# Unsigned conversion on ScalarE in place of a logical shift on VectorE, in the weight conversion of an attention and mixer kernel

## The chip, the cores and the metric

The kernel runs on one core of a Trainium2 chip (trn2). The metric is device time in microseconds of one execution, as the median over runs. Five engines work side by side, each with its own queue of instructions in a fixed order: TensorE (PE, with its weight loads as PEld), VectorE (DVE), ScalarE (ACT), GpSimd (POOL) and SyncE (SP, which here only issues DMAs).

## The reference, cut to what matters

Causal attention with a cumulative bias (4 batches, 8 heads, 576 positions, head size 64) feeds a gated feed-forward layer, and that a mixer over tokens and channels. What matters here are the seven large weight arrays.

```
x = attention(q, k, v, s)                       # (4, 576, 512)
xk, xr = mixes of x and x shifted by one row    # mu_k, mu_r
kk = relu(xk @ w_k) ** 2                        # w_k  512 x 1024
x  = sigmoid(xr @ w_r) * (kk @ w_v)             # w_r  512 x 512, w_v 1024 x 512
h  = relu(x.T @ w_tok1) @ w_tok2                # w_tok1 576 x 256, w_tok2 256 x 576
u  = x + h.T
out = u + relu(u @ w_ch1) @ w_ch2               # w_ch1 512 x 1536, w_ch2 1536 x 512
```

The weights are float64 in memory. Every large product is computed as three products of two parts, a high part (float32r) and what is left of the float32 value (a low part), so each weight is needed as a pair of tiles.

## The kernel before, in words

**Stages.** Batch 0's attention is done in float32, first its first 256 rows (`early`, lines 300 to 328), then the rest (`late`, 346 to 385); batches 1 to 3 use split parts (`scores`, `transposes`, `values`, 265 to 452). The units of the feed-forward layer (`up` 465, `gate` 480, `down` 492, `mix` 454) of a batch run between the attention of the next one. The mixer (`y_transpose` 768, `tok1` 782, `tok2` 795, `ch1` 808, `ch2` 815) comes last and is, from about 575 us on, an almost bare sequence of products on TensorE.

**Weight conversion.** `weight_load` (537) brings a piece of float64 words, seen as pairs of 32-bit integers, into a tile called `raw`; `weight_split` (546) turns it into the two parts. It reads the low and the high word of each number with a step of two words and works in place:

1. ACT, line 549 (recorded at line 74, the helper `copy`): high word times 2 ** -112, as float32.
2. DVE, 550: low word shifted right by 29.
3. DVE, 551: high word shifted left by 3, or-ed with the low word. It waits for 1 and 2.
4. DVE, 552: the sign bit of the high word or-ed in.
5. ACT, 554 (for w_v alone): times one half.
6. ACT, 555: the high part (to `WK`, `WR`, `WV`, `T1`, `T2`, `C1` or the second weights of the channel mixer, which take the places of `WV` and `WR`).
7. POOL, 556 (DVE for w_v): the low part, the difference.

There are 85 pieces: 8 of w_k and 4 of w_r with 512 numbers per partition (in tiles of the pool `wst`, 5 buffers), 16 of w_v with 256, 5 of w_tok1 with 256, 24 of w_ch1 with 256, 4 of w_tok2 with 288, and 24 of w_ch2 with 256 (all these in the pool `xt`, 6 buffers). A buffer comes free with step 7, and the load of a later piece (SP, line 541) waits for it. w_k, w_r and w_v are converted in the first 125 us, w_tok1 and w_ch1 up to about 530 us, w_tok2 and w_ch2 from about 529 to 592 us.

**Order.** `at(place)` gives each part a priority by its place in the program; a planner that simulates the engines with its own costs (`schedule_with_timeline_sim=True`) then fixes the order on each engine. An instruction with another engine or another planned cost can therefore change the order of others. Between 475 and 530 us ACT also runs `up`'s three activations (472 to 474), POOL its difference (475), and `down`'s products (`vd`, line 107) wait for that one.

Of the kernel before, what the change touches and what calls it, by code (L numbers as in the profile page):

```python
# [9 lines left out]
F32R = mybir.dt.float32r  # L10
BF16 = mybir.dt.bfloat16
I32 = mybir.dt.int32
AF = mybir.ActivationFunctionType
ALU = mybir.AluOpType
PSUM = bass.MemoryType.PSUM
# [3 lines left out]
def f32(ap):  # L19
    return ap.bitcast(F32)  # L20
# [3 lines left out]
def attention_moe_mixer(  # L24
# [16 lines left out]
    nc = tc.nc  # L41
# [16 lines left out]
    scale = 1.0 / float(D) ** 0.5  # L58
# [13 lines left out]
    def copy(e, out, in_, scale=1.0):  # L72
        if e == "A":
            nc.scalar.activation(out=out, in_=in_, func=AF.Copy, scale=scale)  # L74
        elif e == "D" and scale == 1.0:
# [45 lines left out]
    HL = qk_p.tile([128, 4 * S], F32, name="HL")  # L121
    VS = v_p.tile([128, NS, 2 * D], F32, name="VS")

    # P^T of the first chunk: key block 0, then what causality leaves of key block 1. Of the
    # second chunk: key block k at BLK[k], the last in columns that its neighbour leaves unused.
    FIRST = QC + 128
    BLK = [CM * k for k in range(NS - 1)] + [CM * (NS - 2) - (128 * (NS - 1) - QC)]
    ft, pt = {}, {}

    # Tiles that batch 0 uses in float32 and the rest as float32r parts.  # L130
    def x_tile(slot, dtype=F32):
        return qk_p.tile([128, 2 * S], dtype, tag=f"X{slot}", name=f"X{slot}").rearrange("p (t s) -> p t s", t=2)

# [6 lines left out]
    X1, X2, PT, VV = {}, {}, {}, {}  # L140
# [13 lines left out]
            nc.scalar.dma_start(out=mu[:, i, :], in_=m.rearrange("(k p) -> p k", p=128))  # L154
        nc.vector.tensor_scalar(out=omu, in0=mu, scalar1=-1.0, scalar2=1.0, op0=ALU.mult, op1=ALU.add)

    # Rows (1, -8 cum_q) and (8 cum_k, 1) whose products add the bias, in float32 for the
    # first chunk of batch 0 and as hi and lo for the rest.
    def bias_rows(cp):
        st = cp.tile([G, S], F32, name="st")  # L160
        nc.sync.dma_start(out=st, in_=s)
        e32 = cp.tile([G, 2, 2, QC], F32, name="e32")
        cum = cp.tile([G, S], F32, name="cum")
        nc.gpsimd.memset(e32[:, 0, 0, :], 1.0)
        nc.gpsimd.memset(e32[:, 1, 1, :], 1.0)
        for c, (a, z) in enumerate(CHS):
            nc.vector.tensor_scalar(out=st[:, a:z], in0=st[:, a:z], scalar1=0.0, scalar2=1.0 / scale, op0=ALU.max, op1=ALU.mult)
            nc.vector.tensor_tensor_scan(
                out=cum[:, a:z], data0=st[:, a:z], data1=st[:, a:z],
                initial=0.0 if c == 0 else cum[:, a - 1:a], op0=ALU.add, op1=ALU.max,  # L170
            )
            if c == 0:
                copy("D", e32[:, 0, 1, :], cum[:, a:z])
                copy("D", e32[:, 1, 0, :], cum[:, a:z], -1.0)
        return cum, e32
# [16 lines left out]
    N1 = (NS - 2) * H  # L192
    NI = N1 + len(items)

    # A visit is a head and the query tiles it covers. Per pair of heads HL holds
    # (q_lo, q_hi, k_lo, k_hi); per head X1 holds (q, k) as [bias rows; zeros; hi] and
    # X2 holds [q_lo; q_hi] and [k_hi; k_lo].
    HLv = HL.rearrange("p (t s) -> p t s", t=4)

    def xs(i):  # L200
# [55 lines left out]
    def softmax(j, P, mx, x):  # L256
        m = min(128, S - 128 * j)
        w = 128 * j + m
        sm = st_p.tile([128, 2], F32, tag="sum", name="sum")
        nc.scalar.activation(out=P[0:m, 0:w], in_=P[0:m, 0:w], func=AF.Exp, bias=mx[0:m, x:x + 1], scale=-1.0, accum_out=sm[0:m, 0:1])  # L260
        nc.vector.tensor_scalar(out=sm[0:m, 0:1], in0=sm[0:m, 0:1], scalar1=1e-9, scalar2=1.0, op0=ALU.add, op1=ALU.mult)  # L261
# [16 lines left out]
        softmax(j, P, mx, x)  # L278
        pst[i, j] = P

    # Batch 0's first chunk, in float32 throughout: HL holds (q, k) of four heads, two more
    # tiles of two each.
    early_at = [(HL, 0, 4)]

    def early_view(h):
# [41 lines left out]
            nc.gpsimd.memset(x[:, 0:1], 0.0)  # L327
            copy("D", x[:, 1:1 + QC], pv)

    # Batch 0's second chunk, in float32 too.  # L330
    late_x, late_v, late_t, late_ps = {}, {}, {}, {}

    def late_load(h):
# [53 lines left out]
    def transposes(i, j):  # L387
# [16 lines left out]
        if j < QC // 128:  # L404
            hi, lo = (ft[i][:, t, :] for t in range(2))
            nc.scalar.activation(out=hi, in_=ps[:, 0:FIRST], func=AF.Copy)
            nc.vector.tensor_tensor(out=lo, in0=ps[:, 0:FIRST], in1=f32(hi), op=ALU.subtract)
# [3 lines left out]
        for r, k0, k1 in ((128, 0, nf), (TAIL, nf, nk)):  # L411
# [9 lines left out]

            nc.scalar.activation(out=view(PT[0]), in_=pv, func=AF.Copy)  # L422
            nc.vector.tensor_tensor(out=view(PT[1]), in0=pv, in1=f32(view(PT[0])), op=ALU.subtract)  # L423

    def values(i, c):
# [24 lines left out]
        tmp = v_p.tile([128, CM], F32, tag="tmp", name="tmp")  # L450
        nc.scalar.activation(out=tmp[a, 0:n], in_=ps[z, :], func=AF.Copy)
        nc.vector.tensor_tensor(out=x[a, 1 + base:1 + base + n], in0=ps[a, :], in1=tmp[a, 0:n], op=ALU.add)

    def mix(b, c, i, p):
# [6 lines left out]
        nc.vector.scalar_tensor_tensor(out=t[:, 0:n], in0=x[:, a:z], scalar=omu[:, i, p:p + 1], in1=t[:, 0:n], op0=ALU.mult, op1=ALU.add)  # L461
        nc.scalar.activation(out=dst[:, 0, p, 0:n], in_=t[:, 0:n], func=AF.Copy)  # L462
        nc.vector.tensor_tensor(out=dst[:, 1, p, 0:n], in0=t[:, 0:n], in1=f32(dst[:, 0, p, 0:n]), op=ALU.subtract)
# [12 lines left out]

    gates = {}

    # sigmoid(z) = (tanh(z / 2) + 1) / 2; the half is in w_v.
    def gate(b, c, m):  # L480
        n = width(c)
        x = act["XR"]
# [54 lines left out]
    def weight_load(key, sw, n, pool, tag):  # L537
        r, k, f = sw.shape
        t = pool.tile([128, n, 2], I32, tag=tag, name="raw")[:, 0:k * f].rearrange("p (k f) t -> p k f t", f=f)
        for r0 in range(0, 128, r):  # L540
            nc.sync.dma_start(out=t[r0:r0 + r], in_=sw.bitcast(I32).rearrange("p k (f t) -> p k f t", t=2))
        raw[key] = t

    # float64 words to float32 bits (scaled by 2 ** -half), then to two 12-bit parts: 2 ** -112
    # on the high word, read as a float32, is the change of exponent bias.
    def weight_split(key, hi, lo, half=0):
        t = raw.pop(key)
        low, high = t[:, :, :, 0], t[:, :, :, 1]
        copy("A", f32(high), f32(high), 2.0 ** -112)
        nc.vector.tensor_scalar(out=low, in0=low, scalar1=29, scalar2=None, op0=ALU.logical_shift_right)  # L550
        nc.vector.scalar_tensor_tensor(out=low, in0=high, scalar=3, in1=low, op0=ALU.logical_shift_left, op1=ALU.bitwise_or)  # L551
        nc.vector.scalar_tensor_tensor(out=low, in0=high, scalar=-2 ** 31, in1=low, op0=ALU.bitwise_and, op1=ALU.bitwise_or)  # L552
        if half:
            copy("A", f32(low), f32(low), 0.5)
        copy("A", hi, f32(low))
        (nc.vector if half else nc.gpsimd).tensor_tensor(out=lo, in0=f32(low), in1=f32(hi), op=ALU.subtract)
# [87 lines left out]
    first = [(nm, W, sw, f) for nm, W, sw, F in (("k", wk, w_k, FF), ("r", wr, w_r, DM)) for f in range(0, F, 128)]  # L644
# [99 lines left out]
    YN = WK[:, o:o + 2 * NS * DH].rearrange("p (t k f) -> p t k f", t=2, k=NS)  # L744
# [18 lines left out]
            nc.sync.dma_start(out=t, in_=y_d[b, 128 * p:128 * p + 128, :])  # L763
            yt[p] = t

    # The low part of the last rows of YN lies below their high part, to meet the high part
    # of w_tok1 (in both halves) in one pass with it.
    def y_transpose(b, h):
        for i in range(NS):
            r = min(128, S - 128 * i)  # L770
# [85 lines left out]
    two = []  # L856
# [63 lines left out]
```

## Time and profile before

| | us |
|---|---|
| median of 3 runs | 928.26 |
| lowest and highest | 923.22, 929.62 |
| span of the profiled execution, first to last instruction | 925.0 |
| TensorE busy in it | 877.3 |
| VectorE busy | 542.4 |
| ScalarE busy | 444.4 |
| GpSimd busy | 297.6 |

The profiled execution is another one than the three timed, and only its span is known; the median of the timed runs lies 3.3 us above that span. All rows are times within the span. Busy times count an instruction from its start to its end; neighbours on an engine overlap a little, so the distance between two starts is the better price of one in a full queue.

### The profile page before, as it was taken

The numbers are of one execution on the slowest core, as the hardware profiler recorded it, in microseconds if no ns is written. First come the engines' busy times: TensorE is split into PE (matmuls) and PEld (weight loads), VectorE is DVE, ScalarE is ACT, GpSimd is POOL, SyncE is SP. The second block draws the span as 40 slices with busy tenths as digits, with TensorE's granted clock in tenths as the row PEclk, the third lists the DMA queues.
The fourth block names the chain that finished last, engine by engine and source line by source line (L and its number), as shares of the span: only waits on it lengthen the run. The fifth ranks groups of instructions, "written<-read, shape, count | busy, mean of one in ns | idle before, by whom it ended". The sixth has DMA issues, their size and how long they took to land.

```text
span 925.0 us, 17127 instructions
## 1 busy us (share of the span) xinstructions
PE 877.3 (95%) x6032; PEld 801.9 (87%) x6032; DVE 542.4 (59%) x1667; ACT 444.4 (48%) x1211; POOL 297.6 (32%) x405
## 2 busy tenths in 40 slices
PE   6869999999899999899999688999999999999998
PEld 4427678998799999899999578999999999999998
DVE  6897776677798567886479967632223222322220
ACT  4667757767777756668376645321112111311120
POOL 5673446644665625554154644200000000000000
PEclk9988999999899999899999899999999999999999
DMA  7952445455643535442125543500010001000000
GB/s 180 267 130 73 121 92 129 108 134 136 143 97 97 116 82 132 94 110 40 52 83 161 160 141 119 181 7 15 15 44 12 15 16 43 12 9 22 18 6 29
DMA packets 57222, 79.61 MB, mean 86 GB/s; under 512 B 6144, under 2 KB 36096, under 8 KB 57136
## 3 DMA queue, kind: packets, MB, share of 16 engines
q1 hardware_dynamic: 55264, 77.92, 32.4%
q8 instruction: 48, 0.79, 0.3%
q10 hardware_dynamic: 1872, 0.59, 0.3%
q14 instruction: 38, 0.31, 0.1%
HBM read 46.67 MB, written 10.03 MB: 61 GB/s over the span
## 4 chain that ended last, share of the span: by engine, by line
PE 71%; DVE 10%; DMA 8%; issue 5%; ACT 3%; POOL 2%; SPq 0%; ACTq 0%; POOLq 0%; DVEq 0%
PE c L107 32%; PE vd L107 7%; PE h L107 7%; PE t L107 4%; PE pv L445 4%; PE r L107 4%; PE t L397 3%; DMA X<-HL 2%; PE s L275 2%; PE s L276 2%; DVE raw L552 2%; PE pv L383 2%; DVE raw L551 1%; DMA raw<-in_moe_w_ch_dram 1%; DVE t L461 1%
## 5 line engine op out<-in xcount | busy, mean ns | idle before, releaser
L107 PE MATMUL c<-XR,C 128*128 128x320 f32 (+1 forms) x1152 | 158.6, 298 | 2.9 <-DVE KK L780 2.1
L107 PEld LDWEIGHTS c<-XR,C 128*128 128x128 f32 x1152 | 155.2, 190 | 4.2 <-DVE KK L780 3.1
L263 POOL TENSOR_SCALAR P<-P,sum 64x576 f32<-64x576 f32 (+4 forms) x160 | 107.4, 675 | 118.1 <-DVE sum L262 56.1
L107 PE MATMUL vd<-KK,WV 128*128 128x256 f32 (+1 forms) x768 | 124.6, 304 | 5.2 <-POOL KK L475 4.9
L107 PE MATMUL h<-XK,WK 128*128 128x256 f32 (+1 forms) x768 | 123.4, 306 | 5.2 <-ACT XK L462 3.6
L107 PEld LDWEIGHTS h<-XK,WK 128*128 128x128 f32 x768 | 109.6, 195 | 9.5 <-ACT XK L462 5.3
L107 PEld LDWEIGHTS vd<-KK,WV 128*128 128x128 f32 x768 | 108.0, 192 | 10.0 <-POOL KK L475 6.1
L260 ACT ACTIVATE P<-P,mx 64x576 f32<-64x576 f32 (+4 forms) x160 | 95.9, 600 | 33.0 <-DVE mx L250 29.3
L107 PE MATMUL c<-KK,WV 128*128 128x256 f32 (+1 forms) x768 | 106.4, 294 | 0.0
L107 PEld LDWEIGHTS c<-KK,WV 128*128 128x128 f32 x768 | 103.0, 188 | 0.0
L779 ACT ACTIVATE KK<-c 128x256 fp32r<-128x256 f32 (+1 forms) x64 | 26.1, 411 | 146.0 <-PE c L107 146.0
L250 DVE CUSTOM_DVE_ANT_0 P<-s,maskc 64x288 f32<-64x288 f32 (+4 forms) x160 | 75.0, 473 | 22.7 <-PE s L276 8.6
L821 DVE TENSOR_TENSOR u<-c,u 128x256 f32<-128x256 f32 (+1 forms) x32 | 14.7, 458 | 123.2 <-PE c L107 123.2
L74 ACT ACTIVATE raw<-raw 128x256 f32<-128x256 f32 (+2 forms) x101 | 46.7, 468 | 43.6 <-DMA raw<-in_moe_w_ch_dram 18.4
L780 DVE SCALAR_TENSOR_TENSOR KK<-c,KK 128x256 fp32r<-128x256 f32 (+1 forms) x64 | 29.1, 456 | 65.5 <-ACT KK L779 65.5
L107 PE MATMUL r<-XR,WR 128*128 128x320 f32 (+1 forms) x384 | 65.6, 306 | 1.4 <-DVE WK L775 1.4
L475 POOL TENSOR_TENSOR KK<-k,KK 128x256 fp32r<-128x256 f32 (+1 forms) x64 | 54.9, 861 | 28.1 <-ACT k L474 27.0
L107 PEld LDWEIGHTS r<-XR,WR 128*128 128x128 f32 x384 | 55.3, 193 | 3.1 <-DVE WK L775 1.6
L107 PE MATMUL c<-XK,WR 128*128 128x320 f32 (+1 forms) x384 | 55.8, 294 | 0.0
L397 PE MATMUL t<-ident,P 128*128 128x128 f32 (+1 forms) x360 | 53.7, 266 | 2.0 <-DVE sum L261 1.1
L107 PEld LDWEIGHTS c<-XK,WR 128*128 128x128 f32 x384 | 52.4, 188 | 0.0
L423 DVE TENSOR_TENSOR PT<-t,PT 128x384 fp32r<-128x384 f32 (+1 forms) x96 | 44.1, 465 | 13.1 <-ACT PT L422 11.7
(109 smaller groups left out, 1521.0 us busy)
## 6 DMA issues: line engine op xcount, KB each, us to landing
X<-HL SPq DMA_DIRECT2D x72, 288.0 KB
raw<-in_moe_w_ch_dram SPq DMA_DIRECT2D x48, 256.0 KB
HL<-in_qk_dram SPq DMA_DIRECT2D x12, 576.0 KB
yt<-y_d SPq DMA_DIRECT2D x16, 288.0 KB
raw<-in_moe_w_k_dram SPq DMA_DIRECT2D x8, 512.0 KB
raw<-in_moe_w_v_dram SPq DMA_DIRECT2D x16, 256.0 KB
VS<-in_v_dram SPq DMA_DIRECT2D x12, 256.0 KB
y_d<-e SPq DMA_DIRECT2D x16, 160.0 KB
```

Of the source, the lines that this page charges most:

```text
L74: nc.scalar.activation(out=out, in_=in_, func=AF.Copy, scale=scale)
L107: nc.tensor.matmul(ps, a, b, start=first and i == 0, stop=last and i == n - 1)
L250: nc.vector.tensor_tensor_reduce(out=P[0:m, c0:c1], in0=ps[0:m, 0:c1 - c0], in1=maskc[0:m, 512 - q0 + c0:512 - q0 + c1], scale=-scale, sca ...
L260: nc.scalar.activation(out=P[0:m, 0:w], in_=P[0:m, 0:w], func=AF.Exp, bias=mx[0:m, x:x + 1], scale=-1.0, accum_out=sm[0:m, 0:1])
L263: nc.gpsimd.tensor_scalar(out=P[0:m, 0:w], in0=P[0:m, 0:w], scalar1=sm[0:m, 1:2], scalar2=1.0, op0=ALU.mult, op1=ALU.mult)
L275: nc.tensor.matmul(ps[0:m, 0:c1 - c0], x1[:, 0, q0:q0 + m], x1[:, 1, c0:c1], start=True, stop=False)
L397: nc.tensor.transpose(ps[0:r, p0 + m * k:p0 + m * k + m], P[0:m, 128 * k:128 * k + r], ident[0:m, 0:m])
L423: nc.vector.tensor_tensor(out=view(PT[1]), in0=pv, in1=f32(view(PT[0])), op=ALU.subtract)
L445: nc.tensor.matmul(ps[:, o:n], vv[0:r, k, :], pair[t], start=(k == 0 and t == 0), stop=(k == nk - 1 and t == 1),)
L475: nc.gpsimd.tensor_tensor(out=kk[:, 1, m, 0:n], in0=t[:, 0:n], in1=f32(kk[:, 0, m, 0:n]), op=ALU.subtract)
L779: nc.scalar.activation(out=hi, in_=ps, func=AF.Relu)
L780: nc.vector.scalar_tensor_tensor(out=lo, in0=ps, scalar=0.0, in1=f32(hi), op0=ALU.max, op1=ALU.subtract)
```

## The change

In `weight_split` the logical shift of the low word on VectorE becomes an activation on ScalarE, on the same words read and written as unsigned integers: the word is converted to float32, multiplied by 2 ** -29 (1 - 2 ** -11), 0.496 is subtracted, and the result is converted back to an unsigned integer. The rest of the chain stays as it was. Six comments also become blank lines; line numbers after the change are 1 to 4 higher.

```diff
+U32 = mybir.dt.uint32
...
+    TOP3 = 2.0 ** -29 * (1.0 - 2.0 ** -11)
+
     def weight_split(key, hi, lo, half=0):
         t = raw.pop(key)
         low, high = t[:, :, :, 0], t[:, :, :, 1]
         copy("A", f32(high), f32(high), 2.0 ** -112)
-        nc.vector.tensor_scalar(out=low, in0=low, scalar1=29, scalar2=None, op0=ALU.logical_shift_right)
+        nc.scalar.activation(out=low.bitcast(U32), in_=low.bitcast(U32), func=AF.Copy, scale=TOP3, bias=-0.496)
         nc.vector.scalar_tensor_tensor(out=low, in0=high, scalar=3, in1=low, op0=ALU.logical_shift_left, op1=ALU.bitwise_or)
```

## Rows read from the trace of the kernel before

**Rows 1.** Page, part 1: busy us, share of the span, instructions.
```profile
PE 877.3 (95%) x6032; PEld 801.9 (87%) x6032; DVE 542.4 (59%) x1667; ACT 444.4 (48%) x1211; POOL 297.6 (32%) x405
```

**Rows 2.** Windows over chosen stretches: length, busy us per engine, granted clock, DMA.
```profile
25.00:50.00 25.00, 22.68 (x59) 10.98 (x58) 23.12 (x66) 18.79 (x46) 17.66 (x15) 1.00 1.06 266
225.00:250.00 25.00, 20.84 (x126) 17.47 (x126) 19.61 (x76) 17.69 (x52) 13.84 (x21) 0.86 0.69 149
...
48.00:68.00 20.00, 13.25 (x42) 5.47 (x39) 19.90 (x43) 12.24 (x28) 14.34 (x14) 0.82 0.51 119
498.00:529.00 31.00, 24.48 (x146) 22.77 (x145) 30.36 (x52) 22.15 (x63) 22.36 (x26) 0.89 0.49 146
529.00:569.00 40.00, 32.81 (x223) 30.12 (x222) 28.19 (x77) 20.03 (x56) 18.00 (x18) 0.96 0.43 135
575.00:925.00 350.00, 346.69 (x2595) 342.51 (x2593) 102.90 (x242) 67.69 (x174) 7.78 (x10) 1.00 0.10 31
```

**Rows 3.** Chain that ended last, in order of time: start us, us, what.
```profile
40.32 7.76 DMA raw<-in_moe_w_r_dram
...
61.48 1.01 DVE raw L551
...
514.63 0.83 DVE raw L550
...
565.58 0.30 DVE raw L550
```

**Rows 4.** Windows of line 550 alone: DVE busy us and count, clock, DMA.
```profile
48.00:68.00 20.00, 3.27 (x6) 0.82 0.51 119
498.00:529.00 31.00, 7.54 (x15) 0.89 0.49 146
529.00:569.00 40.00, 6.38 (x18) 0.96 0.43 135
```

**Rows 5.** Timeline of DVE, two places: start us, us, instruction, shapes.
```profile
58.56 0.41 DVE L550 TENSOR_SCALAR raw<-raw 128x512 int32<-128x512 int32 x1
...
504.92 0.28 DVE L550 TENSOR_SCALAR raw<-raw 128x256 int32<-128x256 int32 x1
505.12 0.41 DVE L552 SCALAR_TENSOR_TENSOR raw<-raw 128x256 int32<-128x256 int32 x1
...
510.10 0.84 DVE L550 TENSOR_SCALAR raw<-raw 128x256 int32<-128x256 int32 x1
```

**Rows 6.** Timeline of POOL, the instruction that runs at 510.10.
```profile
509.99 0.80 POOL L556 TENSOR_TENSOR C<-raw,C 128x256 fp32r<-128x256 f32 x1 [0.83 <-ACT C L74]
```

**Rows 7.** Timeline of ACT: two neighbours.
```profile
499.24 0.42 ACT L74 ACTIVATE raw<-raw 128x256 f32<-128x256 f32 x1
499.56 0.46 ACT L474 ACTIVATE k<-k 128x320 f32<-128x320 f32 x1
```

**Rows 8.** Waits of all engines, 498 to 529: us, times, longest.
```profile
ACT C L74 <- DVE raw L552: 8.7, 9, 1.5
...
PE vd L107 <- POOL KK L475: 4.9, 3, 2.1
```

**Rows 9.** SP's own waits, 477 to 569.
```profile
SPq L541 <- POOL WV L556: 14.4, 6, 5.4
```

**Rows 10.** Windows of 5 us: as in the second group.
```profile
65.00:70.00 5.00, 1.65 (x2) 0.50 (x2) 4.46 (x12) 3.23 (x10) 4.82 (x5) 0.50 0.23 63
...
515.00:520.00 5.00, 3.27 (x13) 2.89 (x12) 4.97 (x9) 3.71 (x11) 3.77 (x6) 0.50 0.45 139
```

**Rows 11.** Timeline of DVE at 540: the first combination behind a fresh load.
```profile
540.38 0.43 DVE L551 SCALAR_TENSOR_TENSOR raw<-raw 128x256 int32<-128x256 int32 x1 [0.17 <-ACT raw L74]
```

**Rows 12.** Groups by form: count, busy us, mean ns, idle before.
```profile
L550 DVE TENSOR_SCALAR raw<-raw 128x256 int32<-128x256 int32 x69 | 26.2, 381 | 19.0 <-DMA raw<-in_moe_w_ch_dram 9.4 <-DMA raw<-in_moe_w_v_dram 5.8 <-DMA raw<-in_moe_w_tok_dram 1.4
...
L74 ACT ACTIVATE raw<-raw 128x256 f32<-128x256 f32 x85 | 36.8, 438 | 37.6 <-DMA raw<-in_moe_w_ch_dram 18.4 <-DMA raw<-in_moe_w_v_dram 9.0 <-DMA raw<-in_moe_w_tok_dram 6.7
...
L74 ACT ACTIVATE raw<-raw 128x512 f32<-128x512 f32 x12 | 8.1, 673 | 4.2 <-DMA raw<-in_moe_w_k_dram 2.1 <-DMA raw<-in_moe_w_r_dram 2.1
```

## The prediction, made before the changed kernel was run

> **What bounds the kernel now.** I read the busy times first. TensorE is busy 877.3 of 925.0 us [rows 1], so whatever the change brings has to come out of the 47.7 us in which it is not, or out of the time that it runs at a lower clock. VectorE has 542.4 us and ScalarE 444.4, so neither bounds the whole, and the share over the span says nothing yet.
>
> Next the windows, stretch by stretch [rows 2]. From 575 us to the end TensorE is busy 346.69 of 350 us at full clock: nothing is won there, and a stage that comes before it moves the end one for one. Three earlier stretches convert weights while TensorE has gaps: 48 to 68 us (13.25 of 20 busy), 498 to 529 (24.48 of 31) and 529 to 569 (32.81 of 40). In the first two VectorE is full, 19.90 of 20 and 30.36 of 31. From 25 to 50 VectorE is nearly full too, but there the DMA share is 1.06, which means that the transfers are the limit.
>
> The chain that ended last says the same [rows 3]: up to 48 us it runs through the load of w_r (7.76 us), then through VectorE's conversion steps and the softmax reduction between them; from 499 to 521 it is almost only lines 550, 551 and 552, and around 540 to 569 these alternate with loads and with GpSimd. So the removed shift stands on the path in two stretches, and that is where its price is to be read. The waits name who suffers: after 500 us the `vd` products wait for GpSimd's difference at line 475 (4.9 us), which is queued among GpSimd's low parts, which wait for ScalarE's high parts, and these for line 552 (8.7 us) [rows 8].
>
> **What the change removes.** One VectorE instruction per piece: six in 48 to 68, fifteen in 498 to 529, eighteen in 529 to 569 [rows 4]. Its price has two ends. In a full queue a shift of 256 numbers takes 0.28 us, and 0.20 from its start to the next (504.92 to 505.12); one of 512 takes 0.41 (at 58.56), with the same overlap 0.33 [rows 5]. But it takes 0.84 us at 510.10, where GpSimd's subtraction runs from 509.99 to 510.79 [rows 6]; it ends 0.15 us after that. Six of the fifteen in 498 to 529 are such long ones. So the fifteen cost at least 15 x 0.20 = 3.0 us, and at most their busy time, 7.54 us. The first holds if the wait for GpSimd passes to the VectorE instruction that comes next, the second if it goes with the shift. I take 3.0: lines 551 and 552 are stretched in the same way, VectorE has one of them ready at nearly every moment there, and GpSimd's 26 instructions stay.
>
> The Trainium skill speaks to this choice (SBUF — State Buffer, Who interferes with whom): a VectorE instruction with two SBUF inputs, or one in a 2-port mode, and a GpSimd instruction that reads SBUF need one pair of ports, whoever starts first keeps it for the whole instruction, and the other blocks. By that rule the wait passes on and the sum has 3.0; without it the 7.54 could go. The shift at 510.10 agrees with it. The same page says that ScalarE waits for no one at SBUF.
>
> For 48 to 68 the ends are 4 x 0.33 + 2 x 0.20 = 1.7 us and the busy time, 3.27; I take 1.7 for the same reason.
>
> **What it adds.** One ScalarE activation per piece, from unsigned to unsigned, a form that the trace does not have. The nearest rows are the copies next to it: 0.32 us from start to start with 256 numbers (499.24 to 499.56) [rows 7]; the mean of one is 0.438, so 0.12 overlap, and 512 numbers with a mean of 0.673 [rows 12] should then take 0.55. I take 0.33 and 0.55. From below, it could not be had under the shift's own 0.20; from above, the slowest engine's instruction of that shape, GpSimd's 0.80 [rows 6], is the far end.
>
> 48 to 68: 4 x 0.55 + 2 x 0.33 = 2.9 us; ScalarE goes from 12.24 to 15.1 of 20 and still has room, so VectorE's 1.7 us are kept. Term: -1.7 (from -3.3 to 0).
>
> 498 to 529: 15 x 0.33 = 5.0 us; ScalarE goes from 22.15 to 27.1. So the stretch cannot shrink by more than 31 - 27.1 = 3.9 us, and ScalarE would then have no gap at all. VectorE gives 3.0; I take 2.5, as the queues are in order and ScalarE's high parts, which wait for line 552, hold up the copies behind them. Term: -2.5 (from -3.9 to 0). What is late next there is ScalarE: behind each added copy stand `up`'s activations (lines 472 to 474), for these wait GpSimd's line 475 and the `vd` products.
>
> 529 to 569: here the buffers turn round. SP's loads wait for GpSimd's low parts (14.4 us for those of w_ch2) [rows 9], the six buffers are filled in turns, and a turn gets longer: line 551 waited for the high word's copy alone (0.17 us idle at 540.38) [rows 11], where the shift lay beside it; now two copies run one after the other ahead of it, 0.33 us more. 18 pieces are three turns of six, 3 x 0.33 = +1.0. Against that VectorE loses shifts that are on the chain only here and there (the one at 565.58 is [rows 3]), so I cost it from 0 to +2 and take +1.0.
>
> The other pieces: before 48 us the DMA hides them (share 1.06) [rows 2]. There ScalarE would go from 18.79 to about 18.79 + 8 x 0.55 = 23.2 of 25, which is the one place in the early part where cover may go. If a w_k buffer comes free later for it, the load of w_r is later by the same; I cost this at 0, and at +2 if the cover is gone. From 75 to 125 the copies lie beside an almost busy TensorE, from 477 to 498 too, and after 575 they are hidden by TensorE altogether.
>
> The sum: -1.7 - 2.5 + 1.0 = -3.2 us on the span of 925.0, so 921.8. The median of the runs lies 3.3 us above that span, and I take that to stay: 921.8 + 3.3 = 925.1, say 925.0 us. With the ends of the terms, this case runs from 921.1 (-3.3 - 3.9 + 0) to 932.3 (0 + 0 + 2 + 2).
>
> One thing has no row: the planner gets other costs on two engines and may order the whole attention part anew. I leave some 4 us for it on either side, an estimate from one gap of TensorE in that part that could come or go with the order (20.84 of 25 us busy in 225 to 250, 4.2 us idle) [rows 2]; it widens every case and favours none.
>
> **The rivals.** *Faster by more than 1%: the waits do go, and the clock comes with them.* The granted clock is 0.50, the lower of its two levels, from 515 to 520 and from 65 to 70, in or right behind TensorE's gaps (1.65 and 3.27 of 5 us busy) [rows 10]. If conversion gets shorter than TensorE's backlog, the gaps close: -6.5 us in 498 to 529 (31 - 24.48), -3.3 in the first stretch, and of the clock (5 x 0.50 + 5 x 0.50 = 5.0 us of full-speed time) about half, -2.5. Sum -12.3, time 916.0. For it: both stretches are VectorE's, and ScalarE's 8.7 us of waiting for line 552 are exactly the gaps that the copies could fill. Against it: 22.15 + 5.0 us on ScalarE do not fit into 24.5.
>
> *Slower by more than 1%: ScalarE becomes the bound in 498 to 529.* If its waits for line 552 stay, the stretch needs 22.15 + 5.0 + 8.7 = 35.8 us, +4.8; `vd` then waits longer behind line 475 and loses another 5 us slice at half clock, +2.5; and the turn of the buffers lengthens for all of the 51 pieces from 475 us on, eight turns and a half, 8.5 x 0.33 = +2.8. Sum +10.1, time 938.4. It decides from the point where more than 3.9 of the 8.7 us of waiting remain. For it: in-order queues, and two engines in one chain. Against it: the planner knows the instruction and can put the copy where ScalarE waits.
>
> *Nothing moves.* What VectorE saves is given to GpSimd's port or to ScalarE's queue in equal parts: 928, inside the same class.
>
> *The new form is dear.* With GpSimd's 0.80 us instead of 0.33, ScalarE gets 15 x 0.47 = 7.1 us more in 498 to 529, 34.2 us in all: the stretch grows by at least 3.2, the first one by 6 x 0.47 = 2.8 at most, and the turns by 3 x 0.8 = 2.4: up to +8.4, 936.7, or over 938 with the planner's 4 us.
>
> **How the numbers follow.** The forecast 0.33, the faster rival 0.30, ScalarE as the bound 0.22, nothing 0.10, a dear form 0.05. About what a measurement of this kernel can tell from no change is 1%, 9.3 us: below 919.0 or above 937.5. Faster: 0.30 and a little of the forecast's spread, 0.31; slower: 0.22 and most of the dear form, 0.26; within: 0.43. The likeliest case's own range is 921 to 932. The range that should hold 8 times in 10 reaches to the faster rival with the planner's 4 us (916.0 - 4 = 912, and 911 for the gap in 529 to 569 that may shrink with it) and to the slower one (938.4, 939).
>
> **What would show it.** Right: VectorE busy less by 26.2 us for the 69 shifts of 256 numbers [rows 12] and by some more for the other 16; ScalarE busy more by about 40 (73 x 0.438 + 12 x 0.673); lines 551 and 552 in 498 to 529 stretched as often as before, more of them with idle time in front that ends with ScalarE; that stretch 1 to 4 us shorter. Wrong: if the first TensorE stage that is full to the end (575 us before) begins over 9 us earlier, the waits did go with the shift; if `vd` waits for line 475 much longer than 4.9 us, ScalarE is the bound; if the stretches without any conversion, 130 to 450 us, take another time, it is the order, and none of my terms; if the new activation takes longer than 0.46 us with 256 numbers, its price was wrong.

## The result, and the profile after

The changed kernel takes 917.15 us (median of 4 runs, 915.82 to 919.12) against 928.75 of the kernel before in the same comparison (4 runs, 923.22 to 929.62). The ratio is 0.9890, with a 95% interval of 0.9865 to 0.9916. That lies within the range of 911 to 939, but 7.9 us below the forecast of 925.0 and near the faster rival's 916.0. The profiled execution has a span of 914.0 us, 11.0 less than that of before.

Busy times of the changed kernel, the answer to [rows 1]:

```profile
PE 869.3 (95%) x6032; PEld 793.9 (87%) x6032; DVE 528.8 (58%) x1582; ACT 468.6 (51%) x1296; POOL 293.9 (32%) x405
```

VectorE has 85 instructions less and ScalarE 85 more, as the diff says. VectorE's busy time fell by only 13.6 us (542.4 to 528.8), less than the 26.2 that the 69 small shifts took [rows 12]. The groups of the conversion's lines, by form (count, busy us, mean ns, idle before), tell a part of why; line 554 is the new activation, 555 and 556 are the old 551 and 552:

```profile
L556 DVE SCALAR_TENSOR_TENSOR raw<-raw 128x256 int32<-128x256 int32 x69 | 40.5, 589 | 0.8
L75 ACT ACTIVATE raw<-raw 128x256 f32<-128x256 f32 x85 | 37.4, 440 | 28.8 <-DMA raw<-in_moe_w_ch_dram 10.7 <-DMA raw<-in_moe_w_v_dram 8.0 <-DMA raw<-in_moe_w_tok_dram 5.3
L555 DVE SCALAR_TENSOR_TENSOR raw<-raw 128x256 int32<-128x256 int32 x69 | 37.1, 538 | 18.7 <-ACT raw L554 16.5 <-issue 1.1 <-POOL C L560 0.6
L554 ACT ACTIVATE raw<-raw 128x256 uint32<-128x256 uint32 x69 | 29.7, 431 | 0.0
```

The activation costs 431 ns, as much as the copy beside it (440): its price was forecast rightly, and the dear form is out. Line 555 now waits 16.5 us for it. In the kernel before the same two lines had these rows:

```profile
L552 DVE SCALAR_TENSOR_TENSOR raw<-raw 128x256 int32<-128x256 int32 x69 | 37.5, 550 | 0.4
L551 DVE SCALAR_TENSOR_TENSOR raw<-raw 128x256 int32<-128x256 int32 x69 | 36.5, 533 | 2.0 <-ACT raw L74 1.5
```

So the sum of both means rose from 1083 to 1127 ns, 3.0 us over the 69 pieces: the waits in them stayed and grew a little. And a shift in a full queue held only 0.20 of its 0.28 us by itself [rows 5], so its busy time was never all to be had. The largest single rise lies outside the conversion, though: the twelve copies of the split values, which the new order puts at other places, took 6.1 us more. Before and after:

```profile
L76 DVE CAST VV<-VS 64x128 fp32r<-64x128 f32 x12 | 5.0, 420 | 2.4 <-PE pv L445 2.4
L77 DVE CAST VV<-VS 64x128 fp32r<-64x128 f32 x12 | 11.1, 929 | 0.1
```

The timeline of VectorE shows a long instruction of line 556 and a short one, and that of GpSimd the subtractions that run beside the long one:

```profile
514.89 0.98 DVE L556 SCALAR_TENSOR_TENSOR raw<-raw 128x256 int32<-128x256 int32 x1
...
518.72 0.43 DVE L556 SCALAR_TENSOR_TENSOR raw<-raw 128x256 int32<-128x256 int32 x1
```

```profile
514.54 2.07 POOL L476 TENSOR_TENSOR KK<-k,KK 128x320 fp32r<-128x320 f32 x2
516.57 1.83 POOL L560 TENSOR_TENSOR C<-raw,C 128x256 fp32r<-128x256 f32 x2
519.76 0.90 POOL L476 TENSOR_TENSOR KK<-k,KK 128x320 fp32r<-128x320 f32 x1 [1.36 <-issue]
```

Between 518.40 and 519.76 GpSimd runs nothing, and the same instruction takes 0.43 instead of 0.98 us. As forecast, the wait for GpSimd passed on to the next VectorE instruction.

The windows that answer to [rows 2] (length, busy us and count of PE, PEld, DVE, ACT, POOL, then clock, DMA share, GB/s):

```profile
48.00:68.00 20.00, 15.38 (x42) 6.45 (x41) 17.95 (x41) 17.52 (x40) 12.34 (x10) 0.62 0.52 142
498.00:529.00 31.00, 25.77 (x159) 23.61 (x157) 26.32 (x40) 27.01 (x81) 23.06 (x27) 0.94 0.54 164
529.00:569.00 40.00, 36.68 (x280) 35.10 (x279) 31.28 (x71) 29.71 (x87) 17.70 (x21) 1.00 0.50 156
...
515.00:520.00 5.00, 4.01 (x27) 3.45 (x25) 4.73 (x8) 5.00 (x16) 3.64 (x5) 1.00 0.59 176
...
564.00:914.00 350.00, 346.66 (x2595) 342.46 (x2594) 102.17 (x237) 70.79 (x185) 8.65 (x11) 1.00 0.10 31
```

The last row against 575 to 925 of before is the plainest one: 346.66 us of TensorE where it was 346.69, 2595 instructions in both. The last 350 us cost the same, so all 11 us were won before them. In 498 to 529 VectorE fell from 30.36 to 26.32 and ScalarE rose from 22.15 to 27.01 (forecast 27.1); in the slice from 515 to 520 it is busy all the time. In 529 to 569 TensorE is busy 36.68 of 40 where it was 32.81, at a clock of 1.00 where it was 0.96.

What TensorE waits for from 498 to 575 us (us in total, times, longest) in the changed kernel:

```profile
PE t L108 <- ACT WK L783: 2.4, 1, 2.4
PE yn L777 <- DVE WK L779: 2.1, 1, 2.1
PE vd L108 <- POOL KK L476: 1.4, 2, 0.9
PE c L108 <- DVE KK L784: 0.9, 1, 0.9
PE vd L108 <- ACT k L473: 0.9, 2, 0.5
PE yn L777 <- ACT e L488: 0.8, 1, 0.8
```

and in the kernel before, behind the 4.9 us of `vd` for GpSimd's KK [rows 8]:

```profile
...
PE c L107 <- DVE KK L780: 2.1, 1, 2.1
PE yn L773 <- DVE WK L775: 1.8, 2, 1.3
PE yn L773 <- ACT e L487: 1.6, 1, 1.6
PE t L789 <- DMA WK<-WK: 1.5, 1, 1.5
PE r L107 <- DVE WK L775: 1.4, 1, 1.4
...
```

The sum falls from 14.0 us (with 0.7 in two short waits that are not shown) to 8.5. It is two things: `vd` waits 3.5 us less for GpSimd, and 5.0 us of single waits for VectorE and for the small DMA behind `y_transpose` (2.1 + 1.5 + 1.4) shrink to 0.9. Two new ones come, both for ScalarE (2.4 and 0.9); the second is of `vd`, which so waits 2.3 us in all where it waited 4.9. The first 498 us brought 1.1 us (the 28th `down` result, at 497.1 before). The clock brought about (0.94 - 0.89) x 31 + (1.00 - 0.96) x 40 = 3.2 us of full-speed time by the windows from 498 to 569, an estimate. That makes 9.8 of the 11.0 us. The 1.1 us of the first 498 are a net: the changed kernel is 3.2 us behind at the 16th result of `down` (353.0 before) and 1.4 ahead at the 24th (463.9), though no weights are converted from 136 to 399 us. The experiments come back to this.

### The profile page after: what moved, and what is told of

Read it like the earlier page. It is cut to its first block, busy times and chain, and to the rows that moved or that the text cites. A ratio compares the mean times of both kernels' runs of the same rounds, so it can differ in the third digit from the quotient of the medians.

```text
span 914.0 us, 17090 instructions
## 1 busy us (share of the span) xinstructions
PE 869.3 (95%) x6032; PEld 793.9 (87%) x6032; DVE 528.8 (58%) x1582; ACT 468.6 (51%) x1296; POOL 293.9 (32%) x405
## 4 chain that ended last, share of the span: by engine, by line
PE 65%; DMA 12%; DVE 8%; issue 6%; POOL 4%; ACT 4%; SPq 1%; ACTq 0%; POOLq 0%; DVEq 0%
PE c L108 32%; PE vd L108 6%; PE h L108 5%; PE t L108 4%; DMA X<-HL 4%; PE pv L446 3%; PE r L108 3%; PE t L398 3%; DMA HL<-in_qk_dram 2%; PE s L357 2%; PE pv L384 2%; DMA raw<-in_moe_w_k_dram 1%; PE s L276 1%; PE s L277 1%; DMA raw<-in_moe_w_ch_dram 1%
## 5 line engine op out<-in xcount | busy, mean ns | idle before, releaser
L108 PE MATMUL h<-XK,WK 128*128 128x256 f32 (+1 forms) x768 | 120.2, 302 | 3.2 <-DVE XK L464 1.5
L108 PE MATMUL vd<-KK,WV 128*128 128x256 f32 (+1 forms) x768 | 120.5, 299 | 2.8 <-POOL KK L476 1.6
L108 PEld LDWEIGHTS h<-XK,WK 128*128 128x128 f32 x768 | 107.0, 191 | 7.2 <-DVE XK L464 2.1
L108 PEld LDWEIGHTS vd<-KK,WV 128*128 128x128 f32 x768 | 105.7, 188 | 6.5 <-POOL KK L476 2.5
L108 PE MATMUL c<-KK,WV 128*128 128x256 f32 (+1 forms) x768 | 106.4, 294 | 0.0
L251 DVE CUSTOM_DVE_ANT_0 P<-s,maskc 64x288 f32<-64x288 f32 (+4 forms) x160 | 75.1, 474 | 27.1 <-PE t L398 9.2
L784 DVE SCALAR_TENSOR_TENSOR KK<-c,KK 128x256 fp32r<-128x256 f32 (+1 forms) x64 | 29.1, 456 | 65.5 <-ACT KK L783 65.5
L75 ACT ACTIVATE raw<-raw 128x256 f32<-128x256 f32 (+2 forms) x101 | 47.2, 469 | 33.1 <-DMA raw<-in_moe_w_ch_dram 10.7
L108 PE MATMUL r<-XR,WR 128*128 128x320 f32 (+1 forms) x384 | 63.5, 304 | 0.0
L555 DVE SCALAR_TENSOR_TENSOR raw<-raw 128x256 int32<-128x256 int32 (+2 forms) x85 | 49.4, 582 | 23.5 <-ACT raw L554 20.6
L556 DVE SCALAR_TENSOR_TENSOR raw<-raw 128x256 int32<-128x256 int32 (+2 forms) x85 | 52.8, 624 | 1.0
```

Source lines behind the costliest of these rows:

```text
L108: nc.tensor.matmul(ps, a, b, start=first and i == 0, stop=last and i == n - 1)
L251: nc.vector.tensor_tensor_reduce(out=P[0:m, c0:c1], in0=ps[0:m, 0:c1 - c0], in1=maskc[0:m, 512 - q0 + c0:512 - q0 + c1], scale=-scale, sca ...
L784: nc.vector.scalar_tensor_tensor(out=lo, in0=ps, scalar=0.0, in1=f32(hi), op0=ALU.max, op1=ALU.subtract)
```

## The experiments

All times stand against runs of the kernel before on the same chip, 926.0 to 926.7 us in the median of each series (against those, if the chips are alike, the changed kernel's 917.15 us is 9 us faster rather than 11.6). I compare ratios; one thousandth is 0.93 us, and a ratio's interval reaches 2 to 5 thousandths to each side. A difference of two ratios is less certain still, so the sizes below are rough.

**Half of the change.** The first question was which pieces bring the gain.

```diff
 # e1: copy for w_tok1, w_ch1, w_tok2, w_ch2 alone; e2: for w_k, w_r, w_v alone
+        if late:   # e2: if not late
             nc.scalar.activation(out=low.bitcast(U32), ..., func=AF.Copy, scale=TOP3, bias=-0.496)
+        else:
+            nc.vector.tensor_scalar(out=low, in0=low, scalar1=29, scalar2=None, op0=ALU.logical_shift_right)
```

> Only the late pieces (w_tok1, w_ch1, w_tok2, w_ch2) get the ScalarE copy; w_k, w_r and w_v keep the VectorE shift. Theory 1 (VectorE is relieved where w_ch1 is converted, TensorE's gaps after 498 us close and the clock with them): 9 to 11 us faster than the kernel before, and TensorE busy in 498 to 569 as after the change. Theory 2 (the planner's new order does it, wherever the edit is): no relation to the whole change; anything from 5 us slower to 10 faster.

Measured: 918.48 us, ratio 0.9925 (0.9895 to 0.9954).

> Only w_k, w_r and w_v get the ScalarE copy; the late pieces keep the VectorE shift. Theory 1: 0 to 3 us faster than the kernel before, and after 498 us the trace of before, moved by that much. Theory 2: this one too can be 5 us slower to 10 faster, and its sum with the late half need not give the whole.

Measured: 918.81 us, ratio 0.9932 (0.9904 to 0.9959).

Either half brings 6 to 7 us, and both together 10; by the times alone, within the noise, the two halves could still add up. The trace of e2 says more. Its late conversion is that of before, yet its gain came late: it was 2.9 us behind before at the 16th `down` result (356 us), 1.5 ahead at the 24th (462) and 7.7 ahead at 594 (the third transfer of `y_transpose`). The order of the instructions in those parts was another. So the theory that the engines' load alone explains the gain failed here, and the planner's order became the rival.

**Neither shift nor copy.** Line 550 goes into 551, which joins the low word's 3 bits with the high word; the high word's own shift by 3 is left out, so what comes out are not the weights.

```diff
-        copy("A", f32(high), f32(high), 2.0 ** -112)
-        nc.vector.tensor_scalar(out=low, in0=low, scalar1=29, scalar2=None, op0=ALU.logical_shift_right)
-        nc.vector.scalar_tensor_tensor(out=low, in0=high, scalar=3, in1=low, op0=ALU.logical_shift_left, op1=ALU.bitwise_or)
+        copy("A", f32(high), f32(high), 2.0 ** -4)
+        nc.vector.scalar_tensor_tensor(out=low, in0=low, scalar=29, in1=high, op0=ALU.logical_shift_right, op1=ALU.bitwise_or)
```

> Neither the VectorE shift nor the ScalarE copy: line 551 shifts the low word itself and or-s the high word in as it is, so the high word's shift by 3 is left out of the computation (and its factor is 2 ** -4). What the removal is worth alone. Theory 1: at least as fast as after the change, 11 to 16 us faster than before; if the ScalarE copy has no price of its own, the same as after within 2 us; if ScalarE bounds 498 to 529 after the change, 3 us or more faster than after, with ScalarE near 22 of 31 us busy there. Theory 2: no order to be expected between this and the change.

Measured: 913.39 us, ratio 0.9863 (0.9817 to 0.9909). Without the copy the kernel is 2.5 us (by ratios) to 3.8 us (by medians) below the changed one. The intervals overlap, so this run alone doesn't show that the copy has a price.

**A first try at the order.** Lines 549 and 550 of before change places.

> The kernel before with its first two conversion steps, which do not depend on each other, written in the other order: the same instructions on the same engines, only the planner's input differs. Theory 1: within 2 us of before. Theory 2: the order alone can move the time by more than 4 us either way, and where it does, TensorE's gaps after 498 us differ from before.

Measured: 926.08 us, ratio 1.0004 (0.9981 to 1.0027). The order came out the same on every engine, so this tried nothing about order; it shows that a kernel with the same work and order measures the same. It also shows how far the single waits vary between two executions of one order: `c` for KK, `t` for the DMA and `r` sum to 2.9 us in e4 (0.7, 0.8, 1.4) and to 5.0 in before, while new ones of 1.4 and 0.6 us come and all its waits together are 13.8 us against 14.0.

**The order alone.** One more tiny instruction at the start makes the planner order all engines anew:

```diff
     copy("D", V0[0:G, 0, 0:1], e32[:, 1, 0, 0:1])
+    copy("D", V0[0:G, 0, 0:1], e32[:, 1, 0, 0:1])
```

How near two orders are was counted on the programs: of 5930 TensorE products, how many stand in a common order (the longest sequence that two programs share). The fourteen kernels fall into two groups of seven. Within a group at least 5506 products stand in a common order, across the groups at most 5246. The counts in the expectations are lower (3857 and 4763 across, 5567 to 5717 within), but part the kernels in the same way.

> The kernel before, with one more copy of the 8x1 column that VectorE copies at the start (some 0.1 us). No other instruction changes, but the planner then orders all engines anew. Theory 'engines' (the gain is the shift that VectorE loses): within 0.4% of before, 924 to 931. Theory 'order' (the planner's order alone is worth as much as the change): the time moves by over 5 us to one side, and TensorE's gaps from 498 to 583 shrink or grow without any change of the work.

Measured: 920.03 us, ratio 0.9934 (0.9914 to 0.9954).

> The kernel before, with two more of the 8x1 copies: a third order of the same work. Theory 'engines': within 0.4% of before, 924 to 931. Theory 'order': another time than the order with one more copy, by some us, and each may lie on either side of before.

Measured: 920.43 us, ratio 0.9935 (0.9912 to 0.9957). This turned out to be no third order but the same as with one more copy, on every engine, so it is a repeat of the first.

The work of before, in another order (5151 of 5930 products in common), takes 6 us less. The busy times from 529 to 569 us of the kernel before with one more copy:

```profile
529.00:569.00 40.00, 36.33 (x266) 34.25 (x265) 32.92 (x87) 21.99 (x63) 16.10 (x19) 0.96 0.41 135
```

TensorE is busy 36.33 us there, like the changed kernel, with VectorE's shift still in place. Its waits from 498 to 575 us:

```profile
PE vd L107 <- POOL KK L475: 5.5, 2, 2.9
...
PE c L107 <- DVE KK L781: 0.4, 1, 0.4
PE t L789 <- ACT WK L775: 0.4, 1, 0.4
PE r L107 <- DVE WK L776: 0.2, 1, 0.2
```

Here the two things come apart. The single waits (KK, the DMA, `r`) are nearly gone, 5.0 us to 0.6 and no DMA, without any change of the work. The wait of `vd` for GpSimd is still 5.5. This is about half of what the order is worth. The other half, 5.3 us, was won between the 16th and the 24th result of `down` (353 to 464 us), where no weights are converted. In the kernel before, three instructions wait there, one behind the other; the last two rows are windows as above:

```profile
368.51 1.26 ACT L74 ACTIVATE HL<-HL 128x576 fp32r<-128x576 f32 x2 [3.86 <-issue]
370.10 0.99 DVE L463 TENSOR_TENSOR XR<-t,XR 128x256 fp32r<-128x256 f32 x1 [4.04 <-ACT XR L462]
372.63 2.44 PE L445 MATMUL pv<-PT,VV 128*128 128x320 f32 x8 [3.27 <-DVE xt L452]
...
370.00:375.00 5.00, 2.37 (x9) 2.29 (x10) 4.80 (x15) 4.37 (x14) 4.74 (x8) 0.65 0.75 152
375.00:380.00 5.00, 5.00 (x24) 4.37 (x23) 2.40 (x12) 2.87 (x12) 3.74 (x5) 0.67 0.31 80
```

ScalarE stands idle ahead of its copy of HL, the queries and keys of the next heads, whose load was issued at 364.2 us; VectorE waits for ScalarE, TensorE for VectorE, and the granted clock is 0.65 and 0.67 in the two slices of 5 us from 370 us on. With one more copy at the start the same two copies run the same 4.3 us after their load was issued (at 363.4 us), but ScalarE has other work until then, its line 462 first:

```profile
363.79 0.42 ACT L462 ACTIVATE XR<-t 128x256 fp32r<-128x256 f32 x1 [0.49 <-DVE t L461]
...
367.66 1.26 ACT L74 ACTIVATE HL<-HL 128x576 fp32r<-128x576 f32 x2
```

All seven kernels of before's group have this wait of TensorE (3.2 to 3.6 us), and none of the other seven; from the 16th to the 17th result of `down` they take 37.8 to 39.0 us, the others 31.9 to 33.9. That ScalarE waits there for the landing of the load is read from the distance between the two, 4.1 to 4.4 us in all fourteen kernels; the profile doesn't name what ended the wait.

**The change in other orders.**

> The changed kernel with the same additional 8x1 copy, so in another order. Theory 'engines': 915 to 919, as the changed kernel, and below each order of the kernel before by 8 us or more. Theory 'order': it spreads as the orders of the kernel before do, and may lie at 920 or more.

Measured: 917.66 us, ratio 0.9924 (0.9902 to 0.9945). With one more copy the changed kernel falls into an order near that of before (5605 in common; without it 5167).

> The kernel before with sixteen more of the 8x1 copies (some 1 us of VectorE at the start): TensorE's order of products is close to that of before (5567 of 5930 in common order), and far from that of the run with one more copy (3857), which took 920.0. Theory 'engines and order' (two kinds of order of the attention part; that of before costs some 6 us): 924 to 929. Theory 'before alone was unlucky' (any other order is better): 919 to 922.

Measured: 928.42 us, ratio 1.0030 (1.0005 to 1.0056).

> The changed kernel with sixteen more copies: TensorE's order is close to that of before (5705 of 5930 in common), not to that of the changed kernel (4763). So the change under nearly the order of before. Theory 'engines and order': the engines' part alone, some 3 us below before, 921 to 925. Theory 'engines' (order is nothing): 915 to 919. If the gain is order alone: 925 to 929.

Measured: 917.97 us, ratio 0.9908 (0.9873 to 0.9942). I had expected 921 to 925 if order and engines added up, and it is faster than that, where the theory of the engines alone had it. In an order near before's the kernel with the shift takes 926 to 928 us and that with the copy 918; in the other order 920 and 917. In the times, the copy's kernels hardly care which it is. The waits of o7 (shift, 498 to 575 us) are those of before again:

```profile
PE vd L107 <- POOL KK L475: 5.2, 3, 2.1
PE c L107 <- DVE KK L796: 2.2, 1, 2.2
...
PE r L107 <- DVE WK L791: 1.4, 1, 1.4
PE t L805 <- DMA WK<-WK: 1.3, 1, 1.3
...
```

and those of o8 (copy, nearly that order) are not:

```profile
PE yn L793 <- DVE WK L795: 2.1, 1, 2.1
PE t L108 <- ACT WK L799: 1.9, 1, 1.9
PE vd L108 <- POOL KK L476: 1.6, 2, 1.0
...
```

**The copy added, the shift kept.**

```diff
         copy("A", f32(high), f32(high), 2.0 ** -112)
+        nc.scalar.activation(out=low.bitcast(U32), in_=low.bitcast(U32), func=AF.Copy, scale=1.0 - 2.0 ** -11, bias=0.0)
         nc.vector.tensor_scalar(out=low, in0=low, scalar1=29, scalar2=None, op0=ALU.logical_shift_right)
```

> The kernel before keeps its shift and gets, behind it in the chain, a ScalarE copy from unsigned to unsigned of the same words (times 1 - 2 ** -11, which leaves the 3 bits and so the result as they are): the added copy alone, nothing removed. My forecast priced the copy in a longer turn of the buffers (+1.0 in 529 to 569) and in ScalarE's room: if that holds, 3 to 10 us slower than before, 930 to 938. If ScalarE's copies are free (its queue has gaps in all stretches and the loads are early enough), within 2 us of before. If order decides, anything from 917 to 935, with other stretches than those of conversion moved.

Measured: 930.31 us, ratio 1.0051 (1.0019 to 1.0083), in an order near that of before (5687).

> Shift kept and ScalarE's copy added, with one more 8x1 copy: TensorE's order is now that of the run of before with one more copy (5717 in common; 920.0 us). The added ScalarE copy cost 4 us under the order of before. If engines and order add up: 920 + 4 = 922 to 926. If the copy's price was the order's: 919 to 921.

Measured: 925.81 us, ratio 0.9989 (0.9969 to 1.0009), in the other order. So the added activation costs 5.1 thousandths in the one order (2.1 against o7, the other kernel near it) and 5.5 in the other, 4.7 (2.0) and 5.1 us. In the other order the intervals of shift and both don't overlap, so there the price is shown.

The ratios side by side:

| | order near before's | the other order |
|---|---|---|
| shift and copy | 1.0051 | 0.9989 |
| shift (before) | 1, 1.0030 | 0.9934, 0.9935 |
| copy (after) | 0.9924, 0.9908 | 0.9890 |
| neither | | 0.9863 |

The copy costs 2.0 us (o7 to both) to 5.1 (shift to both). The shift's removal gives 6.6 us (shift to neither) or 9.2 (both to copy) in the other order, and 11.8 to 13.2 (both to copy) in that of before. The sum of the change is -4.1 us in the other order and -7.0 to -8.5 in that of before (-11.3 between the two kernels with sixteen more copies). The difference between the two orders is about as large as the noise of four ratios, so that order and change don't add up rests on the traces too. They tell it stretch by stretch, in us of the profiled executions; the kernels with the shift are before, e4 and o7, then o1, o3 and e2; with the copy e1, o2 and o8, then the changed one and e7:

| | shift | copy | both | neither |
|---|---|---|---|---|
| 16th to 24th result of `down` (353 to 464 in before), near before's | 110.9, 111.5, 110.9 | 111.4, 110.0, 110.9 | 111.4 | |
| the same, the other order | 105.6, 105.1, 106.4 | 106.3, 104.7 | 106.6 | 105.2 |
| 28th result to the end of w_ch1's conversion (497 to 530), near before's | 32.4, 32.8, 32.4 | 29.0, 29.1, 29.1 | 38.1 | |
| the same, the other order | 32.6, 33.1, 33.3 | 29.4, 30.8 | 37.9 | 27.9 |
| from there to the third transfer of `y_transpose` (530 to 602), near before's | 72.0, 70.7, 72.3 | 64.5, 64.3, 64.9 | 66.8 | |
| the same, the other order (e7, with the shift there: 66.0) | 67.3, 66.6, 65.7 | 65.1 | 65.4 | 68.0 |

Two executions of one order (before and e4, o1 and o3, the changed kernel and e7 up to 523 us) differ by up to 1.6 us in a row. The first stretch follows the order alone. The second follows the conversion alone: in either order the change gives 1.8 to 3.9 us, as the sum of a copy that costs 1.1 to 5.7 and a shift whose removal gives 4.5 to 9.1. In the third, only before, e4 and o7 take 71 to 72 us. In any other late order the shift takes 65 to 67, hardly more than the copy's 64 to 65 and no more than the 68 without either. The programs bear this out. Of 620 products that run from about 490 to 600 us in before, e4 and o7 have the same order; o1, o3 and e2 have one that differs from it in the place of nine; and the four kernels with the copy in all late pieces (the changed one, e1, o2, o8) share a third, with 576 in common with the first.

**The shift kept from 529 us on.**

```diff
+        if shift:   # w_tok2 and w_ch2
+            nc.vector.tensor_scalar(out=low, in0=low, scalar1=29, scalar2=None, op0=ALU.logical_shift_right)
+        else:
             nc.scalar.activation(out=low.bitcast(U32), ..., func=AF.Copy, scale=TOP3, bias=-0.496)
```

> The changed kernel, but w_tok2 and w_ch2 (28 pieces, from 529 us on) keep VectorE's shift. My forecast had the copy cost 1.0 us there (a longer turn of the six buffers): then 915.5 to 917 and faster than the changed kernel by about 1. If the copy helps there too (VectorE was the limit of that stretch), slower than the changed kernel by 1 to 4 us, 918 to 921.

Measured: 913.98 us, ratio 0.9863 (0.9824 to 0.9902): the fastest kernel here that computes the whole, 12 us below before. That it beats the changed kernel too isn't shown. The intervals overlap, and the two programs have the same order on every engine until 523 us, while in the profiles e7 is already 4.3 us ahead at 492 (the 28th `down` result) and only 2.0 at 589. So two executions of identical instructions differ by up to 4.3 us, and e7 lost half of that lead again where it keeps the shift. That the copy costs anything from 529 us on is not seen.

## Why the prediction was right and wrong, point by point

**What bounds the kernel** was right: nothing changed in the last 350 us, and what was won earlier moved the end one for one.

**48 to 68 us, -1.7.** Not seen, though 1.7 us is within the noise of a ratio. Copies for the early pieces alone (e2, 0.9932) are no faster than the kernel before in nearly the same order (o1, 0.9934; 5790 products in common), and copies for the late pieces alone (e1, 0.9925) bring as much as all of them in before's kind of order (o2, 0.9924). The window is busier on TensorE (15.38 against 13.25 us), but its clock was 0.62 against 0.82. The early conversion gets longer with the copy, which the term left out: that of w_v ends at 131.6 to 135.7 us in the seven kernels with early copies and at 123.6 to 129.3 in the seven without.

**498 to 529 us, -2.5.** Nearly right. The last low part of w_ch1 ends at 525.7 instead of 529.9, 4.2 us earlier, of which 1.1 were there at 497: -3.1, within the -3.9 to 0, and the table has the same step, about -3, in both orders. This is the term whose cause is shown. VectorE's wait did pass on to the next instruction; ScalarE's busy time came out as worked out, 27.0. And what was named as the victim, `vd` behind GpSimd's KK, is what got better: 4.9 to 1.4 us. That wait is 4.9 to 5.5 us in all six kernels in which w_ch1 is shifted on VectorE without a copy (before, o1, o3, o7, e2, e4), and 1.3 to 1.6 in all five with the copy alone (after, o2, o8, e1, e7). With both it is 3.1 and 4.1 (o6, e6), and with neither 3.3 (e3), though e3 has the shortest stretch of all. So VectorE's relief alone doesn't explain it.

**529 to 569 us, +1.0.** This is the term that failed. From the end of w_ch1's conversion to the `t` products that open the full last part (at 579.46 before, 568.41 after) the lead grew from 4.2 to 11.0 us: -6.8 instead of +1.0. About 5 us of that came with another late order and not with the shift, by the third stretch of the table: with the shift in place, e2, o1 and o3 take 65.7 to 67.3 us there instead of before's 72.0, and the changed kernel 65.1. The turn of the buffers was no limit either. The waits for the loads of w_ch2 from 529 to 569 us were, in before:

```profile
ACT raw L74 <- DMA raw<-in_moe_w_ch_dram: 9.2, 6, 3.8
DVE raw L550 <- DMA raw<-in_moe_w_ch_dram: 8.0, 3, 4.1
...
```

and in the changed kernel:

```profile
DVE raw L555 <- ACT raw L554: 8.4, 7, 1.8
ACT raw L75 <- DMA raw<-in_moe_w_ch_dram: 4.0, 8, 1.5
...
```

I read this as buffers that came free earlier, with a conversion of w_ch1 that ended 4.2 us earlier. The 8.4 us in which VectorE waits for the new activation are the longer chain that was priced, but none of TensorE's waits in the list further up ends with a step of the conversion. What TensorE waited for were VectorE's other steps and the small DMA, which the forecast didn't look at, as it counted only the conversion's own instructions. Did the shifts hold these steps up? At the end of the stretch of before, VectorE and ScalarE:

```profile
566.92 0.83 DVE L550 TENSOR_SCALAR raw<-raw 128x256 int32<-128x256 int32 x1
567.86 0.77 DVE L551 SCALAR_TENSOR_TENSOR raw<-raw 128x256 int32<-128x256 int32 x1
568.56 0.28 DVE L550 TENSOR_SCALAR raw<-raw 128x256 int32<-128x256 int32 x1
568.76 0.41 DVE L780 SCALAR_TENSOR_TENSOR KK<-c,KK 128x256 fp32r<-128x256 f32 x1
...
567.38 0.42 ACT L74 ACTIVATE raw<-raw 128x256 f32<-128x256 f32 x1
567.70 0.64 ACT L779 ACTIVATE KK<-c 128x256 fp32r<-128x256 f32 x2
```

Line 780 is the one for which the `c` products waited 2.1 us, from 567.1 on. The shift right ahead of it takes 0.20 us from start to start. The long one doesn't count, as line 551 behind it needs ScalarE's copy that ends at 567.80, and line 780 itself needs line 779, which starts at 567.70. So the shifts hold up a tenth of this wait, and in e4, with the same order, the whole wait for KK is 0.7 us. That the shifts cost much here is not shown.

**"It widens every case and favours none."** The planner's 4 us had about the right size, but they were not even-handed. The order of before was a poor one: another order of the same work is 6 us faster. A change that upsets the order could lose little and win much, and the term should have leaned to the faster side. The forecast took its size from a gap at 225 to 250 us; the gap that went lies at 369 to 373, with the low clock behind it, and stood in the same trace. What another order does to it could be found out ahead only with a second order at hand.

**The signs.** Two of the signs of being wrong came: the full last part begins 11.05 us earlier, over the 9 that were named, and the part without conversion took another time (106.3 us from the 16th to the 24th result instead of 110.9), which the prediction itself would have put down to the order. VectorE's busy time fell by 13.6 us instead of over 26, and ScalarE's rose by 24.2 instead of 40, as neighbours overlap. The activation's price, the stretched lines 551 and 552 and the 1 to 4 us in 498 to 529 came as forecast.

**The terms against the pairs.** I had -4.2 us for the shift and +1.0 for the copy. The pairs give -6.6 to -13.2 and +2.0 to +5.1. Both were too small, and the sum of -3.2 is near the -4.1 of the other order because the errors offset each other, which is luck. In the order in which before stood, the change brings twice that, since the late order that comes with it also takes the 5 us in 530 to 602 that the other order takes by itself. That is why order and change don't add up. The time lies within the range in part by luck too. Of the profile's 11.0 us, 3.1 came in 498 to 529, by the way that was forecast; 4.6 came with the order before 464 us, 6.9 behind 530, some 5 of them with the late order, and the changed kernel's first 353 us gave 3.2 back.

**The rivals.** The faster one had the size, mostly by chance, and part of the mechanism: TensorE's waits shrink by 5.5 us, and the clock from 515 to 520 is 1.00 where it was 0.50 [rows 10]. But the first stretch, which it counted with -3.3 and part of the clock's 2.5, brought nothing that shows; 498 to 529 brought -3.1 and not -6.5; and 529 to 569 and the order before 464 us, which it left out, brought most. The slower rival's price for ScalarE exists (5 us, with the shift kept), and ScalarE is full from 505 to 520 us after the change, but its wait for line 552, 8.7 us in 498 to 529, went away, and with it the condition for that case.

**Open.** The four kernels with the copy in all late pieces also share a late order that no kernel with the shift has, so how much of `vd`'s 3.5 us is VectorE's relief and how much the place of the products was not separated; holding the order fixed was not tried. Before 464 us the costly decision is, as far as the traces show, the place of HL's copy in ScalarE's queue; a kernel with that copy alone moved was not run. Which decision costs the 5 us in 530 to 602 isn't known (the places of nine products go with them), nor why the planner takes either.

## What to carry to other kernels

Where a planner sets the order, time the unchanged work in a second order (one redundant tiny instruction was enough) before a gain of one per cent is put down to an engine. Price a moved instruction with two more kernels, one that has both forms and one that has neither: a net of -3 can be -9 and +5. In a stretch where the last engine waits, list what it waits for and see whose queue that stands in. Cut the span at the same results in every kernel and compare the pieces: a piece that the change can't touch and that moves all the same is the order's. And look for an engine that idles ahead of an instruction that waits for a load while others stand behind it.

## What the runs showed of the hardware that was not expected

An activation from unsigned to unsigned integers, with both conversions, takes the time of one from float32 to float32: 431 against 440 ns with 256 numbers, 668 against 674 with 512. And two executions of the same instruction streams drift apart by 2 to 4 us by the middle of the span (e1 lies 2.1 us behind before at 400 us, up to where their orders are the same, and e7 4.3 ahead of the changed kernel at 492), by up to 1.6 us within one stretch of the table. So a stage's gain of under 2 us isn't to be read from one profile each, nor a lead of 4 us over many stages.
